# Later weight loads in the scan, rows two experts ahead, doubled columns, no fillers: six edits to a fused scan, expert and DFT kernel

## The chip, the cores and the metric

The kernel runs on one core of a Trainium2 chip, in one launch. The time is device microseconds of that core. Three runs of the kernel before took 473.55, 471.59 and 469.82 us (median 471.59); the execution whose profile is read here took 473.05, of which 471.3 lie between the first and the last instruction.

## The reference

Three stages follow one another (4 batches, 768 positions, 256 features):

```python
# 1. decaying scan, 8 heads of 32, state of 16, in chunks
M = einsum('bhin,bhjn->bhij', C, B) * exp(cum_i - cum_j) * causal
y = M @ x + (C @ state) * exp(cum)
state = exp(sum(la)) * state + sum_j(B_j x_j * exp(cum_last - cum_j))
# 2. mixture of 8 experts; the choice is sticky along a sequence
e = argmax(logits[b, s]) if s == 0 or sigmoid(x @ w_local) < 0.5 else prev_e
out[b, s] = softmax(logits)[e] * (relu(x @ w1[e]) @ w2[e])
# 3. real part of a 2-D DFT, residual, layer norm, feed-forward layer
u = x + real(fft(fft(x, axis=1), axis=2))
un = (u - mean(u)) / sqrt(var(u) + 1e-6)
result = u + relu(un @ w_ch1) @ w_ch2
```

All of it is float32. The kernel keeps that precision by splitting each matmul operand into a high and a low part, so that one product is three matmuls.

## The kernel before

**The scan** (`phase_a`) runs 12 iterations `i`, six chunks of 128 positions by two pairs of batches; ScalarE's `x1t` (L452) closes an iteration. SP issues the chunk loads (`load`, L242, two chunks ahead), GpSimd builds operands and scatters finished rows into `xs_buf` by expert. In the same program loop SP issues the first expert's weights: `load_w(0)`, `r1` at `i = 5` and `r2` at `i = 7`, and at `i = 9` the tables `fa` and `fb` for the DFT. The order in the program is the order on each engine; SP waits only where a buffer is still in use.

**The experts** (`experts`) are taken in turn, the first of which has one early block of 256 rows and then a block of 128. `ffn` has eight f-groups (L847, 48 matmuls; ScalarE takes the relu `hh`, L851, and DVE the rest `hl`, L852), then a block of 24 matmuls (L860) for each 128 rows; GpSimd scatters the result to `y_tok`. PSUM holds three f-groups. After each f-group (0 to 7) and each row block (8 and up), `hook(i)` puts in work for what comes next: the split of the next expert's weights (`w1h`, `w2h` on ScalarE, `w1l`, `w2l` on DVE, L183 and L186), the transposes `tp` of its rows (L874, hook 7), and the preparation of the last stage's weights, `prep_wch`: a load `rawc`, four DVE operations (L133 to L136), a copy on ScalarE (L140) and two operations on GpSimd. `rawc` and the raw expert weights `r` share two buffers of one pool (`wraw`). `load_x` loads the rows `xn` of the next expert, which come from `xs_buf`, or `xs_part` for the last one. That one is sorted again on the way (`sort_rows`) and runs in two pieces, a block of 128 rows and the rest.

**The transform** follows in the same program. At the turn from the last expert, TensorE computes the DFT of the first batch (`f` L1217, `cps` L1231, `mix` L1247 and L1248). Between these stand fillers, matmuls of 512 columns on `fa` with no reader:

```python
keep_clock(ps1, WARM)   # WARM = 10
stage_a(0, 1)
...
keep_clock(ps1, 5)
```

A filler shows as two records in the trace. Six groups of 512 rows go through the feed-forward layer, while the table `plan` says after which f-group of which group the steps of the next batch (fold on DVE, then `mid`: DFT, residual, norm) are taken.

Of the kernel before, what the change touches and what calls it, by code (L numbers as in the profile page):

```python
# [7 lines left out]
FP32 = mybir.dt.float32  # L8
# [9 lines left out]
NE, F = 8, 1024  # L18
# [9 lines left out]
RW = D + 9  # L28
# [7 lines left out]
)  # L36
GATE = -1.5 * 2.0 ** -23

WARM = 10
CA = {}  # L40
_o = 0
for _n, _w in (
# [10 lines left out]
def tile_kernel(ctx: ExitStack, tc: tile.TileContext, io):  # L53
    nc = tc.nc
    V, A, G, PE, SP = nc.vector, nc.scalar, nc.gpsimd, nc.tensor, nc.sync
# [18 lines left out]
    fa = const.tile([128, 12, 128], FP32, name="fa")  # L74
    fb = const.tile([128, 2, 129], FP32, name="fb")
# [33 lines left out]
    def prep_wch(i, pool):  # L109
        n = 512  # L110
        w = i // 4
        q = i % 4
        if w == 0:
            src = io["wc1"][(q // 2) * 128:(q // 2) * 128 + 128, (q % 2) * n:(q % 2 + 1) * n]
            dst = [t[:, q // 2, (q % 2) * n:(q % 2 + 1) * n] for t in wch[0:2]]
            sh = [128, n]
            raw = wraw.tile([128, n, 2], I32, tag="raw", name="rawc")
            SP.dma_start(out=raw.rearrange("p f t -> p (f t)"), in_=src.bitcast(I32))
        else:
            src = io["wc2"][q * 256:q * 256 + 256, :]  # L120
            dst = [t[:, 2 * q:2 * q + 2, :] for t in wch[2:4]]
            sh = [128, 2, D]
            raw = wraw.tile([128, n, 2], I32, tag="raw", name="rawc")
            SP.dma_start(
                out=raw.rearrange("p (k d) t -> p k (d t)", k=2),
                in_=src.bitcast(I32).rearrange("(k p) d -> p k d", p=128),
            )
            dst = [t.rearrange("p k d -> p (k d)") for t in dst]
        hw, lw = raw[:, :, 1], raw[:, :, 0]
        v = pool.tile([128, n], I32, tag="cv", name="cv")  # L130
        e = pool.tile([128, n], I32, tag="ce_", name="ce_")
        r = pool.tile([128, n], FP32, tag="cr", name="cr")
        V.tensor_scalar(out=e, in0=hw, scalar1=3, scalar2=0x3FFFFFF8, op0=ALU.logical_shift_left, op1=ALU.bitwise_and)  # L133
        V.scalar_tensor_tensor(out=v, in0=hw, scalar=-0x40000000, in1=e, op0=ALU.bitwise_and, op1=ALU.bitwise_or)
        V.tensor_scalar(out=e, in0=v, scalar1=-0x800000, scalar2=None, op0=ALU.bitwise_and)
        V.scalar_tensor_tensor(  # L136
            out=r, in0=lw.bitcast(mybir.dt.uint32), scalar=2.0 ** -52, in1=e.bitcast(FP32), op0=ALU.mult, op1=ALU.mult
        )
        vf = v.bitcast(FP32)
        A.activation(out=dst[0], in_=vf, func=ACTF.Copy)  # L140
        ef = e.bitcast(FP32)
        G.tensor_tensor(out=ef, in0=vf, in1=dst[0], op=ALU.subtract)
        G.tensor_tensor(out=dst[1], in0=ef, in1=r, op=ALU.add)
# [11 lines left out]
            )  # L155
        return regs[j]

    def load_w(e, part=None, static=False):

        i = bass.ds(e if static or e == 0 else expert(e), 1)  # L160
        if part != 1:
            r1 = wraw.tile([128, 2, F], FP32, tag="raw", name="r1")
            SP.dma_start(out=r1, in_=io["w1"][i].rearrange("o (k p) f -> p (o k) f", p=128))
            raws[e, 0] = r1
        if part != 0:
            r2 = wraw.tile([128, 8, D], FP32, tag="raw", name="r2")
            SP.dma_start(out=r2, in_=io["w2"][i].rearrange("o (k p) d -> p (o k) d", p=128))
            raws[e, 1] = r2

# [39 lines left out]
    def keep_clock(pool, n):  # L209

        wps = pool.tile([128, 512], FP32, tag="mm1", name="wps")
        for _ in range(n):
            PE.matmul(out=wps, lhsT=fa[:, 0, :], rhs=fa[:, 0:4, :].rearrange("p n k -> p (n k)"), start=True, stop=True)  # L213
# [7 lines left out]
    def phase_a():  # L221
        with ExitStack() as st:
# [467 lines left out]
            for i, (c, bp) in enumerate(pairs):  # L690
# [7 lines left out]
                if i < 4:  # L698
                    zfill(2 * i)
                    zfill(2 * i + 1)  # L700
                if i in (5, 7):
                    ws = load_w(0, i // 7)
                if i == 9:
                    SP.dma_start(out=fa, in_=io["fa"].rearrange("p (n k) -> p n k", k=128))
                    SP.dma_start(out=fb, in_=io["fb"].rearrange("p (n k) -> p n k", k=129))
                    SP.dma_start(out=rix, in_=io["rix"])
# [130 lines left out]
    def ffn(pools, e, xt_src, evac, hook=lambda i: None, n=CAP):  # L837
        hp, ps1, ps2 = pools
# [4 lines left out]
        for f in range(8):  # L843
            ps = ps1.tile([128, CAP], FP32, tag="mm1", name="mm1")
            terms = [(w, xh, d) for d in range(2) for w in (w1h, w1l)] + [(w1h, xl, d) for d in range(2)]
            for k, (w, x, d) in enumerate(terms):
                PE.matmul(  # L847
                    out=ps[:, 0:n], lhsT=w[:, d, f * 128:(f + 1) * 128], rhs=x[:, d, 0:n], start=(k == 0), stop=(k == 5)
                )
            hf = hh[:, f, 0:n]  # L850
            A.activation(out=hf, in_=ps[:, 0:n], func=ACTF.Relu)  # L851
            V.scalar_tensor_tensor(out=hl[:, f, 0:n], in0=ps[:, 0:n], scalar=0.0, in1=hf, op0=ALU.max, op1=ALU.subtract)  # L852
            hook(f)
# [26 lines left out]
    def load_x(pools, e, xn=None):  # L880

        n = -(-CAPS[e] // 128) * 128
        if xn is not None:
            src = xs_buf.rearrange("(e t) r -> e t r", e=NE)[bass.ds(expert(e), 1), 0:n, :]
            SP.dma_start(out=xn[:, 0:n // 128], in_=src.rearrange("o (t p) r -> p (o t) r", p=128))
            return xn
        xn = pools[0].tile([128, 4, RW], FP32, tag="xn", name="xn")
        if e in SORTED:
            src = xs_part[e][0:n, :].rearrange("(t p) r -> p t r", p=128)
        elif e:  # L890
# [98 lines left out]
    def overflow(pools, nr):  # L989
# [4 lines left out]
        with tc.For_i(1, nr, 1):  # L994
            V.tensor_scalar(out=ro, in0=ro, scalar1=float(CAP), scalar2=None, op0=ALU.add)
            for e in range(NE):
# [3 lines left out]
                past(oo, ro, cnt[:, e:e + 1].to_broadcast([128, 4]))  # L1000
                oi = sm.tile([128, 4], I32, tag="oi", name="oi")
                V.tensor_scalar(out=oi, in0=ro, scalar1=float(e * NTOK), scalar2=None, op0=ALU.add)
                xn = pools[0].tile([128, 4, RW], FP32, tag="xn", name="xn")
                for t in range(4):
                    G.indirect_dma_start(
                        out=xn[:, t, :], out_offset=None, in_=xs_buf,
# [17 lines left out]
    def experts():  # L1024
# [19 lines left out]
                nxt = split_x(pools, xn, out_of[:, 0, :], CAPS[0])  # L1044

        moe_expert(pools, 0, xe, ids_e, early, first, n=EARLY)
        last = NE - 1
        for e in range(NE):
            cur = (xn, *nxt)
            more = e < last  # L1050
            if more:
                xn = load_x(pools, e + 1)

            def hook(i):
                nonlocal nxt, ws, nr
# [11 lines left out]
                if more and i in at:  # L1067
                    next(ws, None)
                    if i == at[-1]:
                        next(ws, None)  # L1070
                        ws = load_w(e + 2) if e + 2 < NE else None
                if i == 7 and more:
                    nxt = split_x(pools, xn, out_of[:, e + 1, :], CAPS[e + 1])
                if (e, i) == (0, 5):
                    prep_wch(0, sm)
                if i == 8 and 0 < e < last:
                    prep_wch(e, sm)
                if (e, i) == (last - 1, 11):
                    prep_wch(7, sm)

# [46 lines left out]
    def transform(lead):  # L1127
# [257 lines left out]
        load_z(1)  # L1385
        sq = sm.tile([128, 1], FP32, tag="sq", name="sq", bufs=1)
        A.activation(out=sq, in_=ident[:, 0:1], func=ACTF.Sqrt)
        keep_clock(ps1, WARM)
        stage_a(0, 1)
        correct(0)  # L1390
        for k2 in range(4):
            stage_b(0, k2)
        keep_clock(ps1, 5)
        for k in range(4):
            add_rows(0, k, G if k else V)
        add_mix(0, 0)
        for k in range(1, 5):
# [13 lines left out]
        run(1, 1)  # L1411

        plan = {
# [3 lines left out]
        }  # L1417
        for g, b in ((2, 2), (3, 3)):
            for k, v in (
# [132 lines left out]
```

## Time and profile before

| | us |
|---|---|
| three runs | 473.55, 471.59, 469.82 |
| profiled execution | 473.05 |
| its span, first to last instruction | 471.3 |
| TensorE busy (PE) | 432.4 (92%) |
| VectorE (DVE) / ScalarE (ACT) / GpSimd (POOL) busy | 274.5 / 183.7 / 152.7 |
| mean granted TensorE clock | 0.955 |

The scan fills the span to about 98 us, the experts to 288, the transform the rest. An engine's busy time says little by itself; the chain of waits follows the last instruction back from releaser to releaser, and the windows give busy time and granted clock of a stretch (1.00 is 2.4 GHz, 0.50 is 1.2 GHz). "PE" are matmuls, "SPq" the DMA issues of SP.

### The profile page before, as it was taken

What the parts mean: (1) busy time and instruction counts of PE and PEld (TensorE: products, weight loads), DVE (VectorE), ACT (ScalarE), POOL (GpSimd) and SP (SyncE); (2) the same over time, 40 slices, a digit from 0 to 9 for tenths busy, and PEclk for the clock granted to TensorE, in tenths of its full rate; (3) what the DMA queues carried; (4) which work ended last, traced back from release to release, by engine and by line L of the source; (5) the groups of instructions that cost most, each with busy time, mean ns of one, the idle gap of its engine ahead of it and who ended that gap; (6) DMA issues with size and microseconds to landing.
All of it is one profiled execution on the core that took longest, in us unless ns stands there. A gap on an engine that the chain in (4) does not pass through costs nothing.

```text
span 471.3 us, 8949 instructions
## 1 busy us (share of the span) xinstructions
PE 432.4 (92%) x3455; PEld 379.0 (80%) x3455; DVE 274.5 (58%) x738; ACT 183.7 (39%) x407; POOL 152.7 (32%) x195
## 2 busy tenths in 40 slices
PE   8798688799899999987989999989999999999996
PEld 4576565469779898986979996668989899998986
DVE  5677577664675657656464453494664578564241
ACT  2354344424344545645353232333240443333130
POOL 2247745431205280622414322342601361400000
PEclk9999799799789999999898799999999999999999
DMA  8799501127364455457351042300131200010101
GB/s 273 258 325 328 186 25 49 66 74 259 116 208 158 148 196 185 149 190 234 118 198 63 19 146 64 139 22 2 56 124 35 78 25 23 2 47 0 46 3 49
DMA packets 33372, 55.22 MB, mean 117 GB/s; under 512 B 3240, under 2 KB 22473, under 8 KB 33320
## 3 DMA queue, kind: packets, MB, share of 16 engines
q1 hardware_dynamic: 29800, 46.28, 29.9%
q0 software_dynamic: 3008, 8.00, 4.9%
q8 instruction: 29, 0.48, 0.4%
q10 hardware_dynamic: 512, 0.28, 0.2%
q14 instruction: 23, 0.19, 0.1%
HBM read 42.05 MB, written 12.63 MB: 116 GB/s over the span
## 4 chain that ended last, share of the span: by engine, by line
PE 78%; DVE 7%; DMA 6%; ACT 5%; issue 2%; another core or an unknown queue 1%; SPq 0%; ACTq 0%
PE mm L860 30%; PE mm L847 23%; PE tl L498 4%; PE wps L213 3%; DMA xn<-xs_buf 3%; PE tp L874 3%; PE g L414 2%; PE f L1217 2%; PE yb L445 2%; DMA xn<-xs_part 2%; PE mb L262 2%; ACT x1t L452 1%; PE yb L434 1%; PE g L262 1%; PE cps L1231 1%
## 5 line engine op out<-in xcount | busy, mean ns | idle before, releaser
L852 DVE SCALAR_TENSOR_TENSOR hl<-mm,hh 128x512 fp32r<-128x512 f32 (+9 forms) x128 | 70.1, 562 | 55.4 <-ACT hh L851 54.6
L851 ACT ACTIVATE hh<-mm 128x512 fp32r<-128x512 f32 (+9 forms) x128 | 62.5, 495 | 83.3 <-PE mm L847 83.1
L860 PE MATMUL mm<-w2h,hh 128*128 128x256 f32 (+3 forms) x224 | 65.5, 292 | 0.0
L860 PE MATMUL mm<-w2l,hh 128*128 128x256 f32 (+3 forms) x224 | 64.3, 287 | 0.0
L860 PE MATMUL mm<-w2h,hl 128*128 128x256 f32 (+3 forms) x224 | 64.3, 287 | 0.0
L961 POOL DMA_INDIRECT y_tok<-y,ids x26 | 32.7, 1257 | 91.2 <-ACT y L960 70.0
L847 PE MATMUL mm<-xh,w1h 128*128 128x128 f32 (+8 forms) x160 | 52.3, 335 | 3.6 <-DVE hl L852 2.8
L860 PE MATMUL mm<-c2h,hh 128*128 128x256 f32 x192 | 54.5, 284 | 0.0
L860 PE MATMUL mm<-c2h,hl 128*128 128x256 f32 x192 | 53.8, 280 | 0.0
L860 PE MATMUL mm<-c2l,hh 128*128 128x256 f32 x192 | 53.8, 280 | 0.0
L847 PE MATMUL mm<-xh,w1l 128*128 128x128 f32 (+8 forms) x160 | 51.5, 330 | 0.0
L860 PEld LDWEIGHTS mm<-w2h,hh 128*128 128x128 f32 (+3 forms) x224 | 42.2, 188 | 0.1
L847 PE MATMUL mm<-xl,w1h 128*128 128x128 f32 (+8 forms) x160 | 40.4, 334 | 1.9 <-DVE xl L877 1.9
L860 PEld LDWEIGHTS mm<-w2l,hh 128*128 128x128 f32 (+3 forms) x224 | 42.1, 188 | 0.1
L860 PEld LDWEIGHTS mm<-w2h,hl 128*128 128x128 f32 (+3 forms) x224 | 41.9, 187 | 0.2
L847 PE MATMUL mm<-xh,c1h 128*128 128x512 f32 x96 | 39.5, 411 | 0.6 <-ACT xh L876 0.6
L847 PE MATMUL mm<-xh,c1l 128*128 128x512 f32 x96 | 38.0, 396 | 0.0
L186 DVE TENSOR_TENSOR w2l<-r,w2h 128x1024 fp32r<-128x1024 f32 (+1 forms) x18 | 21.7, 1212 | 27.5 <-ACT w2h L183 27.5
L847 PEld LDWEIGHTS mm<-xh,w1h 128*128 128x128 f32 x160 | 31.6, 197 | 7.1 <-DVE hl L852 5.0
L860 PEld LDWEIGHTS mm<-c2l,hh 128*128 128x128 f32 x192 | 36.4, 190 | 0.1
L860 PEld LDWEIGHTS mm<-c2h,hh 128*128 128x128 f32 x192 | 36.3, 189 | 0.1
L860 PEld LDWEIGHTS mm<-c2h,hl 128*128 128x128 f32 x192 | 36.0, 188 | 0.0
(279 smaller groups left out, 866.2 us busy)
## 6 DMA issues: line engine op xcount, KB each, us to landing
r<-in_w_dram SPq DMA_DIRECT2D x16, 1024.0 KB
rawc<-in_wc_dram SPq DMA_DIRECT2D x8, 512.0 KB
out_dram<-o SPq DMA_DIRECT2D x24, 128.0 KB
home<-y_tok SPq DMA_DIRECT2D x3, 768.0 KB
xs_buf<-scr SPq DMA_DIRECT2D x8, 265.0 KB
c1h<-in_x_dram SPq DMA_DIRECT2D x4, 512.0 KB
home<-y_tok SPq DMA_DIRECT2D x4, 512.0 KB
xn<-xs_buf SPq DMA_DIRECT2D x3, 530.0 KB
```

Source lines behind the costliest of these rows:

```text
L186: V.tensor_tensor(out=l_[:, x:y], in0=r_[:, x:y], in1=h[:, x:y], op=ALU.subtract)
L213: PE.matmul(out=wps, lhsT=fa[:, 0, :], rhs=fa[:, 0:4, :].rearrange("p n k -> p (n k)"), start=True, stop=True)
L262: PE.matmul(out=ps[:, 0:w], lhsT=wrm[:, 0:128], rhs=wrm[:, 0:w], start=True, stop=True)
L414: PE.matmul(out=gp[q][:, u].rearrange("p h i -> p (h i)"), lhsT=lds[c]["bt"][r:r + 32, 2 * bp + u, :], rhs=ch[r:r + 32, u].rearrange("p q ...
L445: PE.matmul(out=yb[32 * h:32 * h + 32, g, 128 * u:128 * u + 128], lhsT=xts[i][:, u, 4 * g + h, :], rhs=m[:, u, 4 * g + h, :], start=(c == ...
L498: PE.matmul(out=tl[:, 128 * g:128 * g + 137], lhsT=x1t[:, g, u, :], rhs=ca[:, o:o + 137], start=(g == 0), stop=(g == 1), skip_group_check= ...
L847: PE.matmul(out=ps[:, 0:n], lhsT=w[:, d, f * 128:(f + 1) * 128], rhs=x[:, d, 0:n], start=(k == 0), stop=(k == 5))
L851: A.activation(out=hf, in_=ps[:, 0:n], func=ACTF.Relu)
L852: V.scalar_tensor_tensor(out=hl[:, f, 0:n], in0=ps[:, 0:n], scalar=0.0, in1=hf, op0=ALU.max, op1=ALU.subtract)
L860: PE.matmul(out=ps[0:m, :], lhsT=h[:, f, t * 128:t * 128 + m], rhs=w[:, f, :], start=(k == 0), stop=(k == 23))
L874: PE.transpose(ps[d][:, t * 128:(t + 1) * 128], src(t, d), ident)
L961: w = G.indirect_dma_start(out=y_tok, out_offset=bass.IndirectOffsetOnAxis(ap=ids[0:m, t:t + 1], axis=0), in_=y[0:m, :], in_offset=None, b ...
```

## The change

It has six parts.

1. In the scan, `load_w(0)` moves from `i = 5, 7` to `i = 6, 8`, and it, `fa` and `fb` are held: GpSimd writes one element of the target buffer in its own order, and the DMA waits for that write.
2. `load_x(e + 2)` is issued at the start of expert `e`, where `load_x(e + 1)` was; the pool has three such buffers for it.
3. In a 128-row `ffn`, each L847 matmul streams its 128 columns twice, into 256 columns of PSUM; only the first 128 are read.
4. `prep_wch(0)` leaves expert 0; 0 to 5 are taken one expert later than 0 to 6 were, and 6 joins expert 1, ahead of `load_w(3)`.
5. At the turn, the first ten fillers go, and five become four.
6. In `plan`, the first step of `mid(1)` moves from after f-group 3 to after f-group 4 of group 0; all twelve are taken by (0, 9) as before.

```diff
@@ prep_wch
-        r = pool.tile([128, n], FP32, tag="cr", name="cr")
+        r = pool.tile([128, n], FP32, tag="cr", name="cr", bufs=1)
@@
+    def held(t):
+        G.memset(t, 0.0)
+
-    def load_w(e, part=None, static=False):
+    def load_w(e, part=None, static=False, late=False):
@@ after each of r1 and r2 is allocated, before its DMA
+            if late:
+                held(r1[0:1, 0, 0:1])
@@ phase_a
-                if i in (5, 7):
-                    ws = load_w(0, i // 7)
+                if i in (6, 8):
+                    g = load_w(0, i // 8, late=True)
+                    ws = g if i == 6 else ws
                 if i == 9:
+                    for t in (fa[0:1, 0, 0:1], fb[0:1, 0, 0:1]):
+                        held(t)
@@ ffn
+            q = 2 if n == 128 else 1
                 PE.matmul(
-                    out=ps[:, 0:n], lhsT=w[:, d, f * 128:(f + 1) * 128], rhs=x[:, d, 0:n], start=(k == 0), stop=(k == 5)
+                    out=ps[:, 0:q * n].rearrange("p (q n) -> p q n", q=q), lhsT=w[:, d, f * 128:(f + 1) * 128],
+                    rhs=x[:, d, 0:n].unsqueeze(1).to_broadcast([128, q, n]), start=(k == 0), stop=(k == 5),
                 )
@@ load_x
-        xn = pools[0].tile([128, 4, RW], FP32, tag="xn", name="xn")
+        xn = pools[0].tile([128, 4, RW], FP32, tag="xn", name="xn", bufs=3)
@@ experts
         moe_expert(pools, 0, xe, ids_e, early, first, n=EARLY)
+        xn1 = load_x(pools, 1)
         for e in range(NE):
             if more:
-                xn = load_x(pools, e + 1)
+                xn = xn1
+            if e + 2 < NE:
+                xn1 = load_x(pools, e + 2)
@@ hook
                         next(ws, None)
+                        if e == 1:
+                            prep_wch(6, sm)
                         ws = load_w(e + 2) if e + 2 < NE else None
-                if (e, i) == (0, 5):
-                    prep_wch(0, sm)
                 if i == 8 and 0 < e < last:
-                    prep_wch(e, sm)
+                    prep_wch(e - 1, sm)
@@ transform
-        keep_clock(ps1, WARM)
         stage_a(0, 1)
-        keep_clock(ps1, 5)
+        keep_clock(ps1, 4)
@@ plan
-            (0, 0): ((1, 0, 1),), (0, 1): ((1, 0, 1), (1, 1, 1)), (0, 2): ((1, 1, 1),), (0, 3): ((1, 2, 1),),
-            (0, 4): ((1, 2, 2),), (0, 5): ((1, 2, 1),), (0, 6): ((1, 2, 1),), (0, 7): ((1, 2, 2),),
-            (0, 8): ((1, 2, 3),), (0, 9): ((1, 2, 2),), (1, 0): ((1, 2, 1),), (1, 1): ((1, 2, 1),), (1, 3): ((1, 2, 1),),
+            (0, 0): ((1, 0, 1),), (0, 1): ((1, 0, 1), (1, 1, 1)), (0, 2): ((1, 1, 1),), (0, 4): ((1, 2, 1),),
+            (0, 5): ((1, 2, 2),), (0, 6): ((1, 2, 1),), (0, 7): ((1, 2, 2),), (0, 8): ((1, 2, 3),),
+            (0, 9): ((1, 2, 3),), (1, 0): ((1, 2, 1),), (1, 1): ((1, 2, 1),), (1, 3): ((1, 2, 1),),
```

The lines of the kernel after stand 7 to 15 further down. On SP, from the end of the scan's loads on, before (`r` are expert weights, `L242` chunk loads):

```order
L163 DMA r_698<-in_w_dram 128x2x1024
L242 DMA c2h<-in_ct_dram 128x512
L242 DMA c2h<-in_bt_dram 128x512
L242 DMA c1l<-in_x_dram 128x1024
L242 DMA c2l<-in_bn_dram 128x512
L167 DMA r_916<-in_w_dram 128x8x256
L704 DMA fa<-in_fa_dram 128x1536
L705 DMA fb<-in_fb_dram 128x258
L706 DMA rix<-in_rix_dram 128x8
```

and with the change:

```order
L249 DMA c2h<-in_ct_dram 128x512
L249 DMA c2h<-in_bt_dram 128x512
L249 DMA c1l<-in_x_dram 128x1024
L249 DMA c2l<-in_bn_dram 128x512
L168 DMA r_814<-in_w_dram 128x2x1024
L174 DMA r_1021<-in_w_dram 128x8x256
L714 DMA fa<-in_fa_dram 128x1536
L715 DMA fb<-in_fb_dram 128x258
L716 DMA rix<-in_rix_dram 128x8
```

The four loads of the last chunk now stand ahead of both weight loads.

On DVE, at the end of expert 1 and the start of expert 2, before:

```order
L133 TENSOR_SCALAR ce__1998<-rawc 128x512
L134 SCALAR_TENSOR_TENSOR cv<-rawc,ce__1998 128x512
L135 TENSOR_SCALAR ce__1998<-cv 128x512
L136 SCALAR_TENSOR_TENSOR cr<-rawc,ce__1998 128x512
L186 TENSOR_TENSOR w2l<-r_1858,w2h 128x1024 x2
L852 SCALAR_TENSOR_TENSOR hl<-mm_2114,hh 128x448
L899 SCALAR_TENSOR_TENSOR tk<-xu,out_of 128x4
L913 TENSOR_SCALAR lead<-tk 128x4
L852 SCALAR_TENSOR_TENSOR hl<-mm_2127,hh 128x448
```

and with the change:

```order
L132 TENSOR_SCALAR ce__1995<-rawc 128x512
L133 SCALAR_TENSOR_TENSOR cv<-rawc,ce__1995 128x512
L134 TENSOR_SCALAR ce__1995<-cv 128x512
L135 SCALAR_TENSOR_TENSOR cr<-rawc,ce__1995 128x512
L193 TENSOR_TENSOR w2l<-r_1852,w2h 128x1024 x2
L132 TENSOR_SCALAR ce__2073<-rawc 128x512
L133 SCALAR_TENSOR_TENSOR cv<-rawc,ce__2073 128x512
L134 TENSOR_SCALAR ce__2073<-cv 128x512
L135 SCALAR_TENSOR_TENSOR cr<-rawc,ce__2073 128x512
L864 SCALAR_TENSOR_TENSOR hl<-mm_2123,hh 128x448
```

The four operations of the second `prep_wch` (L132 to L135) stand between `w2l` and the first `hl` of expert 2.

On SP, at the end of expert 0 and in expert 1, before (a TENSOR_LOAD reads the number of an expert):

```order
L163 DMA r_1856<-in_w_dram 128x2x1024
L167 ISA
L167 DMA r_1858<-in_w_dram 128x8x256
L895 ISA
L895 DMA xn<-xs_buf 128x4x265
L152 TENSOR_LOAD who
L885 ISA
L885 DMA xu<-xs_buf 128x4x265
L118 DMA rawc<-in_wc_dram 128x1024
L152 TENSOR_LOAD who
L163 ISA
L163 DMA r_2076<-in_w_dram 128x2x1024
```

and with the change:

```order
L168 DMA r_1850<-in_w_dram 128x2x1024
L174 ISA
L174 DMA r_1852<-in_w_dram 128x8x256
L151 TENSOR_LOAD who
L907 ISA
L907 DMA xn<-xs_buf 128x3x265
L151 TENSOR_LOAD who
L897 ISA
L897 DMA xu<-xs_buf 128x4x265
L117 DMA rawc<-in_wc_dram 128x1024
L123 DMA rawc<-in_wc_dram 128x2x512
L168 ISA
L168 DMA r_2082<-in_w_dram 128x2x1024
```

`xn` of expert 3 now comes ahead of `rawc`, and a second `rawc` ahead of `r`.

## Rows read from the trace of the kernel before

**Rows 1.** The page, part 4: shares of the chain of waits that ended last.
```profile
PE 78%; DVE 7%; DMA 6%; ACT 5%; issue 2%; another core or an unknown queue 1%; SPq 0%; ACTq 0%
```

**Rows 2.** Windows: stretch, length, busy us (count) per engine, granted clock, DMA share, GB/s.
```profile
44.40:53.30 8.90, 5.06 (x94) 3.61 (x90) 5.24 (x18) 3.14 (x9) 6.45 (x10) 1.00 0.87 316
53.30:61.60 8.30, 7.59 (x93) 5.86 (x93) 4.83 (x12) 2.82 (x8) 4.98 (x8) 0.59 0.14 49
61.60:68.20 6.60, 5.00 (x101) 3.60 (x90) 5.06 (x18) 4.09 (x10) 2.58 (x4) 1.00 0.01 2
118.00:125.00 7.00, 7.00 (x36) 7.00 (x36) 2.79 (x5) 0.52 (x2) 0.00 (x0) 0.51 0.24 77
...
224.00:227.30 3.30, 2.72 (x13) 2.75 (x14) 0.95 (x3) 1.03 (x2) 0.00 (x0) 0.50 0.12 46
...
264.90:271.70 6.80, 6.80 (x34) 6.80 (x33) 0.87 (x3) 0.83 (x3) 0.32 (x1) 0.50 0.00 0
288.00:305.50 17.50, 17.50 (x74) 10.28 (x73) 4.85 (x22) 5.75 (x16) 4.90 (x11) 1.00 0.39 122
```

**Rows 3.** Chain of waits (start us, us, work): 256-row block; last expert 128-row block.
```profile
101.15 6.42 PE mm L847 x48
107.56 2.83 PE mm L860 x24
...
267.42 4.85 PE mm L860 x24
```

**Rows 4.** Chain of waits, expert 0 with its 128-row block.
```profile
113.44 3.31 PE mm L847 x30
...
119.28 4.26 DMA rawc<-in_wc_dram
...
125.30 0.42 ACT hh L851 x2
...
126.70 1.73 DVE w2l L186
128.43 1.14 DVE ids L899
...
130.76 11.14 PE mm L847 x43
```

**Rows 5.** Timeline of DVE, experts 1 and 2: start us, us of one or more instructions.
```profile
152.51 1.23 DVE L186 TENSOR_TENSOR w2l<-r,w2h 128x1024 fp32r<-128x1024 f32 x1 [1.44 <-ACT w2h L183]
...
165.51 0.15 DVE L899 SCALAR_TENSOR_TENSOR ids<-xn,out_of 128x3 int32<-128x3 int32 x1
```

**Rows 6.** Timeline of ACT, second f-group of expert 2.
```profile
156.60 1.05 ACT L183 ACTIVATE w1h<-r 128x1024 fp32r<-128x1024 f32 x1
```

**Rows 7.** Waits of PE, 98 to 310 us: total us, times, longest.
```profile
PE tp L874 <- DMA xn<-xs_buf: 4.9, 2, 3.3
...
PE tp L874 <- DMA xn<-xs_part: 2.2, 1, 2.2
```

**Rows 8.** Chain of waits from the last expert into the transform.
```profile
288.12 8.58 PE wps L213 x20
...
301.17 4.29 PE wps L213 x10
305.46 0.90 PE tp L874 x7
```

**Rows 9.** Timeline of ACT at the turn.
```profile
288.69 1.28 ACT L1387 ACT_TABLE_LOAD   x1
```

**Rows 10.** Chain of waits, first group of the transform: PE is released by this.
```profile
314.64 0.21 DVE home L1178
...
326.46 1.38 PE mm L847 x6
```

**Rows 11.** Chain of waits in the scan: the steps without a known releaser.
```profile
51.32 1.96 another core or an unknown queue
...
81.67 2.50 another core or an unknown queue
```

More of the change, by code (lines that the diff above doesn't have):

```diff
@@ L37 @@
 GATE = -1.5 * 2.0 ** -23
-WARM = 10
 CA = {}
@@ L166, in load_w @@
             r2 = wraw.tile([128, 8, D], FP32, tag="raw", name="r2")
+            if late:
+                held(r2[0:1, 0, 0:1])
             SP.dma_start(out=r2, in_=io["w2"][i].rearrange("o (k p) d -> p (o k) d", p=128))
@@ L1002, in overflow @@
                 V.tensor_scalar(out=oi, in0=ro, scalar1=float(e * NTOK), scalar2=None, op0=ALU.add)
-                xn = pools[0].tile([128, 4, RW], FP32, tag="xn", name="xn")
+                xn = pools[0].tile([128, 4, RW], FP32, tag="xn", name="xn", bufs=3)
                 for t in range(4):
```

## The prediction, before the run

> **What bounds the kernel now.** I read the chain of waits first, then the windows at each place where the chain leaves TensorE, then the timelines there. The chain is 78% TensorE [rows 1]: a change pays where it takes out a step of the chain that is not matmul, or a stretch in which the matmuls run at the lower clock. The windows [rows 2] show both. In the scan, 44.4 to 53.3, TensorE is busy 5.06 of 8.90 us and the DMA engines 87% of the time, with 0.59 of the clock just after; 118 to 125, 224 to 227.3 and 264.9 to 271.7 run at 0.50, the 1.2 GHz level, and three stretches of 3.4 us like the second start at 131.7, 247.8 and 316.1. A matmul block of 24 takes 4.85 us at that level and 2.83 at full clock [rows 3], so each us of such a stretch holds about half a us that could come back.
>
> The profiled execution took 473.05 us, 1.5 more than the median of 471.59. The sum is made against 473.05.
>
> **Expert 0: the first `prep_wch` leaves.** Its load is issued when DVE has freed the buffer, and DVE then stands in front of it: from 119.28 (`rawc`, 4.26) to 125.30, where the last two relus run [rows 4], are 6.02 us. What takes its place is the last f-group, which needs the DVE product that ends there: 6 matmuls at 3.31/30 = 0.11 us, and a relu, 0.95 together. GpSimd's two tensor operations of the prep go too; beside them `w2l` took 1.73 and `ids` 1.14 [rows 4] where later experts show 1.23 and 0.15 [rows 5]: 1.5 more, if that is why. 6.02 - 0.95 + 1.5 = 6.6. The half-clock stretch after the idle time (3.4 us from 131.7) is worth 1.7. If the stretch of 118 to 125 stays, the row block costs 2 of this back, so the ends are 4.6 and 8.3; I take **8.0**, since DVE's wait is what emptied TensorE.
>
> **Expert 1 to 2: prep 6 arrives.** Eight preps remain eight; 1 to 5 keep their places as 0 to 4. Prep 6 stands behind `w2l`, its load issued when prep 0 frees the buffer, some 5 us before DVE gets there, so I cost its landing at nothing. It adds four DVE operations (2.2 us beside row blocks) and moves `load_w(3)`'s first half from that buffer to the one that `w2l` frees, at 153.74 [rows 5]. ScalarE cuts that half into `w1h` at 156.60 [rows 6]; a load that lands 4.3 us after issue, as the 512 KB of `rawc` did, or 6, since 512 KB more take 1.7 at the 316 GB/s of the scan [rows 2], makes it 1.4 to 3.1 late. Behind `w1h` on ScalarE stand the relus, and TensorE can run two f-groups of some 1.2 us ahead on three PSUM buffers. Cost 0 to 4, with a clock loss behind it; I take **-1.2**.
>
> **Rows two experts ahead.** PE's transposes wait 4.9 us in two places for `xn` from `xs_buf` and 2.2 in one from `xs_part` [rows 7]. Issued an expert earlier, each load has over 20 us of cover, and in SP's queue nothing new stands behind it that is due sooner: its third buffer has been free for an expert. All 7.1 go, and with them the two half-clock stretches behind the idle times (224 [rows 2] and 247.8), 1.7 each: **+10.5**, between 7.1 and 10.5.
>
> **128-row blocks streamed twice.** 96 matmuls grow from 128 to 256 columns. The 128-column ones are 0.110 apart [rows 4]; at 256 columns the rows show 2.83/24 = 0.118 and 6.42/48 = 0.134 [rows 3]. So 96 x 0.008 to 0.024 is 0.8 to 2.3 lost, nearer the lower end because the second figure holds the start of its block; half of it lies in expert 0. In the last expert, 264.9 to 271.7 at 0.50 [rows 2] begins inside such a block after a wait for DVE; if the denser stream holds the clock, 3.4 come back. If not, only the loss stays. I take **+2.4**, between -2.3 and 2.6. The Trainium skill (TensorE: Matmul & The Clock Gate, section Back-to-back issue gap) gives 134 cycles for 128 columns and 262 for 256 at full clock, an estimate of 53 ns more each and 5 us in all. The rows disagree, with 8 to 24 ns more.
>
> **The turn.** Twenty filler records, 8.58 us, go from the path [rows 8]; TensorE stands at full clock there [rows 2]. The DFT's inputs are ready before 288, and the next limit is ScalarE's table load, 1.28 us from 288.69 [rows 9], which delays the copy of `f` by some 0.5. Of the later fillers one in five goes, 0.86 of 4.29; but the rows for the transposes at 305.46 become ready just then, so that fifth was free. 8.58 - 0.5 = 8.1, plus 0.2 for a little slack: **+8.3**, between 6.4 (a half-clock stretch of 3.4 us follows) and 8.6.
>
> **The plan.** `stage_a(1, 0)` moves behind one more f-group. TensorE is released at 314.85 by DVE's fold [rows 10]. But that f-group needs a PSUM buffer which DVE frees at about the same time, so the wait mostly changes its name: **+0.5**, between -1 (the steps now crowd in front of the next transposes) and 1.7.
>
> **The scan.** 2.9 MB (two loads of 1024 KB, one of 768, one of 129) leave the time before 53 us, when the DMA engines are full. The gap in TensorE at 51.32 (1.96) ends as they drain, but it has no known releaser, and 81.67 has a like one of 2.50 [rows 11] when the scan's loads are long done. Iterations 6 and 7, 44.4 to 53.3 to 61.6, took 17.2 us where iteration 8 takes 6.6 at full clock [rows 2]: 4 to 5 could go, half of it clock. Later landing costs nothing while its cover lasts: `r1` is first cut at the end of iteration 7, and its hold stands in GpSimd's queue in iteration 6, behind two scatters; `r2` and `fa` have two iterations and more. If `r1` went only at the end of iteration 6, 53.3, it would land some 4.3 to 6 later, still within iteration 7. I take **+3.0**, between 0 and 6.
>
> 8.0 - 1.2 + 10.5 + 2.4 + 8.3 + 0.5 + 3.0 = 31.5, and 473.05 - 31.5 = **441.5**. Against the median it could be 1.5 lower; I leave that for small waits not seen. All low ends together give 4.6 - 4 + 7.1 - 2.3 + 6.4 - 1 + 0 = 10.8, or 462; all high ends 8.3 + 0 + 10.5 + 2.6 + 8.6 + 1.7 + 6 = 37.7, or 435.
>
> **The rivals.**
> (a) *The clock does not come back.* The stretches move instead of vanishing: 1.7 + 3.4 + 3.4 = 8.5 of the sum are clock, and a stretch at expert 2 and one at the turn would take 3.4 more: 441.5 + 8.5 + 3.4 = 453, or 449 with part of it. For it: every one of these stretches follows a wait, and new waits come. Against: most of the waits before them go. 0.21, of which 0.03 with so many new waits that less than 1% is gained.
> (b) *The scan was slow by DMA alone*, and the plan's stretch goes as well: 441.5 - 3 - 1.2 = 437, down to 434. The second gap with idle rings speaks against it. 0.11.
> (c) *A doubled matmul costs its columns.* At 512 columns six take 1.38 [rows 10], 0.230 each; by the slope from 0.118, 0.056 per 128 columns, 96 cost 5.4 instead of 1: 446. The 0.110 at 128 columns, far above half of 0.118, speaks against it. 0.05. This is the way that the Trainium skill's rule above would go.
> (d) *Slower: the turn without its fillers leaves TensorE at half clock into the transform.* A block of 24 then costs 2.02 more [rows 3]. Losing the 31.5 and 5 more takes 18 such blocks, some 87 us at the lower level; the longest stretch in the rows is 6.8. It decides only if the clock stays down for most of the 166 us that follow: 441.5 + 36.4 = 478. 0.03. The Trainium skill (TensorE: Matmul & The Clock Gate, section Why this matters for your kernels) advises against idle gaps between matmul bursts, which speaks for fillers; no row shows this turn without them.
> (e) *The holds do nothing*, because the gap at 51.32 was never DMA: 444.5. It lies inside the forecast, which has 0.60 with 437 to 447.
>
> **How the numbers follow.** The range 435 to 453 leaves out the lowest quarter of (b), the upper third of (a), and (d), under 0.2 together. A change of 1% (4.7 us) is about what these runs can tell. Faster is all but (d) and the tail of (a): 0.94; same 0.03; slower 0.03.
>
> **What would show it.** In the profile after: no DVE wait for `rawc` in expert 0 and expert 1 starting near 124 less what the scan gave; no wait of the transposes for `xn`; clock 1.00 through the last expert's 128-row block; transposes 17.3 - 8.3 = 9 us after the last expert's final matmul; at expert 2 a late `w1h` of 1 to 4 us; scan iterations 4 to 7 near 6 us each. I am wrong if half-clock stretches stand behind new places, if `w1h` of expert 2 stops TensorE for over 4 us, or if the scan waits for `r1`.

## The result, and the profile after

| | before | change |
|---|---|---|
| runs beside each other, us | 469.37 to 473.55, median 470.70 | 443.98, 448.41, 449.04, 451.18, median 448.73 |
| ratio | | 0.9492 [0.9399, 0.9585] |
| profiled execution, us | 473.05 | 449.04 |
| its span, us; granted clock | 471.3; 0.955 | 447.2; 0.977 |
| another chip (C below), median us | 462.34 | 438.13, ratio 0.9529 [0.9469, 0.9589] |

The ratios here and below leave out runs of either kernel that lie over 1.5% above its fastest one, so they differ from the quotient of the medians, and ratios from different chips cannot be compared.

The kernel is 22 us faster, where 30 were forecast against the median. The spans differ by 24.1, and the question is where the missing 7 are. The page's shares of the chain, which answer to [rows 1], show what has left: DMA fell from 6% to 1%.

```profile
PE 79%; DVE 8%; ACT 6%; issue 3%; DMA 1%; another core or an unknown queue 1%; POOL 1%; ACTq 0%; DVEq 0%
```

The chain of waits of the changed kernel (start us, us, work; L858, L872, L886 are the old L847, L860, L874) answers to [rows 3, 4, 8]. From the early block to the transform:

```profile
104.65 6.19 PE mm L858 x48
...
116.67 1.45 PE mm L858 x12
...
118.36 1.07 ACT w1h L190
...
119.51 1.22 DVE w1l L193
...
127.13 10.40 PE mm L858 x48
137.53 0.88 PE tp L886 x8
...
149.61 5.51 DMA r<-in_w_dram
...
161.97 0.66 PE tp L886 x6
...
183.26 0.66 PE tp L886 x6
...
217.87 0.88 PE tp L886 x8
...
236.62 0.88 PE tp L886 x8
...
251.24 3.85 PE mm L858 x30
255.09 2.81 PE mm L872 x24
257.90 6.32 PE mm L858 x48
...
269.82 1.34 PE f L1232 x12
...
273.97 1.34 PE f L1232 x12
...
283.07 0.56 PE tp L886 x3
```

The chain has no `rawc` in expert 0, no `xn` at the last transposes and no filler between 273.97 and 283.07, and a block of 24 in the last expert's 128 rows takes 2.81 instead of 4.85. One DMA step is new: the weights `r` of expert 3, issued at 149.61, landing 5.51 later and cut within expert 2. PE's waits from 98 to 310 us (us in total, times, longest) no longer have the two `xn` lines of [rows 7]; the longest are now:

```profile
PE mm L858 <- DVE hl L864: 4.0, 6, 1.6
PE ps L934 <- DVE ahead L929: 1.5, 1, 1.5
```

`ahead` is a vector operation in expert 2, part of sorting the last expert's rows. Before, this wait was short, and one of expert 1 for the low part of its rows (`xl`) stood there that is gone now:

```profile
PE mm L847 <- DVE xl L877: 1.9, 1, 1.9
...
PE ps L922 <- DVE ahead L917: 0.3, 1, 0.3
```

The table goes by stretches of the chain, between events that both kernels have (us; a plus is a gain). The second pair of traces was taken later, before and change on one chip (C); that execution of the kernel before was faster than the eleven others of it there.

| stretch | forecast | first pair | second pair |
|---|---|---|---|
| start to early block | +3.0 | 101.15 to 104.65: -3.5 | 90.20 to 93.29: -3.1 |
| to expert 1's transposes for expert 2 | +8.0 | 40.75 to 32.88: +7.9 | 38.24 to 32.87: +5.4 |
| two experts on | -1.2 | 43.42 to 45.73: -2.3 | 43.53 to 45.66: -2.1 |
| to the last expert's transposes | +10.5, in part in the next row | 61.23 to 53.36: +7.9 | 58.78 to 53.16: +5.6 |
| to the first DFT | +2.4 | 37.50 to 33.20: +4.3 | 36.23 to 33.22: +3.0 |
| DFT to transposes (the turn) | +8.3 | 21.41 to 13.25: +8.2 | 21.41 to 13.24: +8.2 |
| the rest | +0.5 | 165.84 to 164.13: +1.7 | 164.41 to 164.06: +0.4 |
| sum | 31.5 | 24.1 | 17.3 |

The stretches at the 1.2 GHz level add up to 40.9 us in the trace before and 20.4 in the one after (14.0 to 17.4, 55.0 to 61.8, 89.1 to 99.3: all in the scan). At most half of such a stretch is lost, so at most 10.2 of the 24.1 are clock. In the second pair it is 13.7 against 6.8, at most 3.4 of 17.3. Taken off in full, that leaves 13.9 us in both pairs; the rest of a pair's gain may be clock.

### The profile page after: what moved, and what is told of

It is laid out like the page before. It is cut to its first block, busy times and chain, and to the rows that moved or that the text cites. A ratio compares the mean times of both kernels' runs of the same rounds, so it can differ in the third digit from the quotient of the medians.

```text
span 447.2 us, 8888 instructions
## 1 busy us (share of the span) xinstructions
PE 415.7 (93%) x3433; PEld 366.6 (82%) x3433; DVE 272.9 (61%) x738; ACT 184.0 (41%) x407; POOL 151.9 (34%) x199
## 4 chain that ended last, share of the span: by engine, by line
PE 79%; DVE 8%; ACT 6%; issue 3%; DMA 1%; another core or an unknown queue 1%; POOL 1%; ACTq 0%; DVEq 0%
PE mm L872 30%; PE mm L858 27%; PE tl L505 4%; PE g L421 3%; PE tp L886 2%; PE f L1232 2%; PE yb L452 2%; PE mb L269 2%; PE g L269 1%; ACT x1t L459 1%; PE yb L441 1%; DMA r<-in_w_dram 1%; PE cps L1246 1%; DVE hl L864 1%
## 5 line engine op out<-in xcount | busy, mean ns | idle before, releaser
L872 PE MATMUL mm<-w2h,hh 128*128 128x256 f32 (+3 forms) x224 | 63.3, 283 | 0.0
L872 PE MATMUL mm<-w2h,hl 128*128 128x256 f32 (+3 forms) x224 | 62.6, 279 | 0.0
L872 PE MATMUL mm<-w2l,hh 128*128 128x256 f32 (+3 forms) x224 | 62.5, 279 | 0.0
L872 PE MATMUL mm<-c2h,hh 128*128 128x256 f32 x192 | 54.5, 284 | 0.4 <-DVE o L1344 0.4
L858 PE MATMUL mm<-xh,w1h 128*128 128x256 f32 (+7 forms) x160 | 51.2, 329 | 3.1 <-DVE hl L864 2.4
L872 PE MATMUL mm<-c2l,hh 128*128 128x256 f32 x192 | 53.6, 279 | 0.0
L872 PE MATMUL mm<-c2h,hl 128*128 128x256 f32 x192 | 53.6, 279 | 0.0
L858 PE MATMUL mm<-xh,w1l 128*128 128x256 f32 (+7 forms) x160 | 49.8, 320 | 0.0
L858 PE MATMUL mm<-xh,c1h 128*128 128x512 f32 x96 | 39.0, 406 | 2.2 <-DVE hl L864 1.6
L872 PEld LDWEIGHTS mm<-w2l,hh 128*128 128x128 f32 (+3 forms) x224 | 39.6, 177 | 0.1
L872 PEld LDWEIGHTS mm<-w2h,hh 128*128 128x128 f32 (+3 forms) x224 | 39.6, 177 | 0.1
L872 PEld LDWEIGHTS mm<-w2h,hl 128*128 128x128 f32 (+3 forms) x224 | 39.5, 176 | 0.2
L858 PE MATMUL mm<-xl,w1h 128*128 128x256 f32 (+7 forms) x160 | 38.4, 321 | 0.0
L858 PE MATMUL mm<-xh,c1l 128*128 128x512 f32 x96 | 37.5, 391 | 0.0
L872 PEld LDWEIGHTS mm<-c2h,hh 128*128 128x128 f32 x192 | 36.1, 188 | 0.8 <-DVE o L1344 0.6
L872 PEld LDWEIGHTS mm<-c2l,hh 128*128 128x128 f32 x192 | 36.1, 188 | 0.1
L872 PEld LDWEIGHTS mm<-c2h,hl 128*128 128x128 f32 x192 | 36.1, 188 | 0.0
L858 PEld LDWEIGHTS mm<-xh,w1h 128*128 128x128 f32 x160 | 30.2, 188 | 6.8 <-DVE hl L864 5.4
```

Of the source, the lines that this page charges most:

```text
L858: PE.matmul(out=ps[:, 0:q * n].rearrange("p (q n) -> p q n", q=q), lhsT=w[:, d, f * 128:(f + 1) * 128], rhs=x[:, d, 0:n].unsqueeze(1).to_b ...
L872: PE.matmul(out=ps[0:m, :], lhsT=h[:, f, t * 128:t * 128 + m], rhs=w[:, f, :], start=(k == 0), stop=(k == 23))
```

## The experiments

The experiments ran on three chips. Runs of the kernel before had a median of 471.29 us on chip A, like those above, of 462.15 on chip B and of 462.34 on chip C. Times from different chips are therefore compared by stretches of the trace.

### The holds and the scan

```diff
-                if i in (6, 8):
-                    g = load_w(0, i // 8, late=True)
-                    ws = g if i == 6 else ws
+                if i in (5, 7):
+                    ws = load_w(0, i // 7)
@@
-                    for t in (fa[0:1, 0, 0:1], fb[0:1, 0, 0:1]):
-                        held(t)
```

> The change without its part on the scan: the first expert's weights and the tables are issued at iterations 5, 7 and 9 as before, without the holds. Theory (the holds buy nothing, and what the scan lost in the profile of the change was the clock, which differs from run to run): the median stays within 2 us of the change's 448.7, the scan's iterations 4 to 7 take 29.5 us as in both profiles, and the gap of 2 us at iteration 6 stays. Rival A (the prediction's: full DMA rings slow the scan): 3 to 6 us slower, 452 to 455. Rival B (the late loads themselves cost the scan the 3.5 us): 445.

449.03 us (447.21 to 450.66) on chip A, ratio 0.9654 [0.9580, 0.9728]: the change's time within its spread. The pause of iteration 6 is there in both. Iterations 4 to 7 take 30.80 us, not the 29.5 expected; 10.2 us of half clock lie there, where both traces of the first pair have 6.8. Chain of waits without the holds:

```profile
51.84 1.96 another core or an unknown queue
53.88 0.61 ACT x1t L459
```

and of the change:

```profile
53.76 2.02 another core or an unknown queue
55.86 0.61 ACT x1t L459
...
83.97 2.61 another core or an unknown queue
```

A second try shifted every later TensorE instruction, in case the pauses came from where the program stands in memory:

```diff
+            warm(24, 32)   # 24 small matmuls at the start of the scan
```

> The change with 24 more matmuls of 32 columns, on zeros and without a reader, at the start of the scan, to shift what follows in TensorE's instruction stream by some 96 instructions. For the two gaps of the scan that have no releaser (about 2.0 us at iteration 6 and 2.5 us at iteration 10, at the same place of the program in all six traces so far). Theory (they hang on the place in TensorE's instruction stream): both move to another iteration, or vanish. Rival (they hang on what the iterations do, the scatters of GpSimd for one, or on data): both stay at iterations 6 and 10.

It took 452.57 us in its one execution, and the pauses were gone. But it ran on chip B, and there they are gone in every trace, those with the unshifted program too. It tells nothing of the shift. Nor is it clear that TensorE was the engine to shift. In both pauses the profile shows ScalarE standing still, here in the kernel before, though the matmuls that it reads from had ended at 51.00 and 81.99 (in brackets its idle time; "remote" is a releaser that the profile does not know):

```profile
53.36 0.60 ACT L452 ACTIVATE x1t<-yb 128x512 f32<-128x512 f32 x1 [2.04 <-remote]
...
84.19 0.17 ACT L557 ACTIVATE f__1272<-mb 128x4 f32<-128x4 f32 x1 [2.53 <-remote]
```

So the change and the kernel before were run with a trace each on chip C:

> The changed kernel itself, unaltered, to be compared with the three other runs of this call on one chip. If the change's gain is the same everywhere, the ratio to the kernel before is 0.94 to 0.96. If the scan's two pauses (2.0 us at iteration 6, 2.6 us at iteration 10) belong to the chip and not to the program, they are there or not there alike in this run and in the kernel before of this call.

> The kernel before, for its trace on the same chip as the changed one. Theory (the pauses in the scan come with the chip or the execution, not with what the rings carry): its scan shows the pauses where the changed kernel's does, and the scan's length differs from the changed kernel's by no more than a half-clock stretch (3.4 us times a half each) explains. Rival (the rings' load makes them): the pauses are in this kernel and not in the changed one.

The change took 438.13 us (437.24 to 440.17). The kernel before took 454.56 in the one execution profiled, and 462.34 in the median of the eleven beside it (456.42 to 465.31). Neither trace has a pause: from the fourth `x1t` to the eighth, the four iterations 4 to 7, pass 24.05 us before and 24.08 after. In the first pair they took 29.70 and 29.49. The windows of iteration 6 (length, busy us (count) of PE, PEld, DVE, ACT, POOL, granted clock, DMA share, GB/s) settle what the rings have to do with it. The kernel before, chip C:

```profile
43.20:49.90 6.70, 4.90 (x100) 3.51 (x90) 5.73 (x19) 3.05 (x9) 5.76 (x10) 1.00 1.06 383
```

the change, same chip:

```profile
44.20:50.90 6.70, 4.84 (x96) 3.52 (x90) 5.72 (x19) 3.04 (x10) 5.76 (x11) 1.00 0.46 107
```

the change, first pair:

```profile
46.87:55.86 8.99, 5.00 (x95) 3.61 (x90) 5.16 (x18) 3.14 (x9) 6.60 (x12) 0.95 0.59 179
```

With the DMA engines at 1.06 the iteration takes 6.70 us, with 0.46 the same 6.70, and with 0.59 in the first pair 8.99. The load of the rings does not make the pause, and taking it away buys nothing; the traces of the first pair and of chip A have the pauses, none from chips B and C. What makes them was not found.

The scan's loss of 3.5 and 3.1 us begins ahead of the holds. In the first pair the change is 2.4 us late at the first `x1t` (16.56 before, 18.95 after) and still 2.4 at the end of the second pause. Of these, 0.7 are the first loads (the first six matmuls of the chain take 4.80 us before and 5.49 after), and the other 1.7 the half-clock stretch from 14.0. In the second pair it is 0.95 late at the first `x1t` (4.27 and 5.21 us for the six) and 0.97 at 80 us. What is left, 1.1 and 2.1 us, is lost where the half-clock stretch at the scan's end lies: 10.2 us with the change and 6.8 before in the first pair, 6.8 and none in the second. The kernel with the fillers back (below), whose scan is that of the change, starts its early block at 92.07, 1.2 earlier, with 3.4 us of half clock there. On chip A the kernel without the holds starts it at 102.96, three others with them at 101.80, 105.09 and 105.82, one sooner and two later. Whether they have a hand in the stretch at the scan's end stays open: it measures 10.2 us in all four traces with pauses and holds and 6.8 in the two without holds; on chips B and C it measures 0 to 6.9 in six with them (the shifted kernel aside), and the one without has none.

### Rows two experts ahead, undone

```diff
-        xn1 = load_x(pools, 1)
@@
-                xn = xn1
-            if e + 2 < NE:
-                xn1 = load_x(pools, e + 2)
+                xn = load_x(pools, e + 1)
```

> The change with the rows loaded one expert ahead, as before. Theory (a wait for the rows and the clock it costs): the waits of the transposes for the rows return, 7 us, with two half-clock stretches, 9.4 us slower than the change, 458. Rival (the rows would land in time now that other loads have moved): no more than 2 us slower.

455.21 us (449.37 to 456.28) on chip A, ratio 0.9745 [0.9618, 0.9871], some 6 us more than the change, where 9.4 were expected. PE's waits, 98 to 310 us, have the two lines again:

```profile
PE tp L886 <- DMA xn<-xs_buf: 2.8, 2, 1.7
PE tp L886 <- DMA xn<-xs_part: 1.3, 1, 1.3
```

The three steps cost 4.1 us of waiting, and the stretch to the last transposes 57.6 instead of 53.4, 4.2 more, with no half-clock stretch in it. So the wait is what this part removes, and the clock comes on top in some executions.

### Doubled columns, undone

```diff
-            q = 2 if n == 128 else 1
+            q = 1
```

> The change with the 128-row blocks streamed once. Theory (the dense stream keeps the clock in the last expert's block): a half-clock stretch of 3.4 to 6.8 us returns there and the kernel is 1 to 3 us slower, less some 1 us that the columns cost: 450 to 452. Rival (the clock held because the waits ahead of the block are gone): no half-clock stretch, and 1 us faster, 447.7, since 96 matmuls go back from 0.12 to 0.11 us.

449.21 us (446.69 to 454.13) on chip A, ratio 0.9662 [0.9541, 0.9784]: as a time, no difference that these runs can tell, and less than the 450 to 452 expected. The windows of the last expert's 128-row block show what is behind it:

```profile
247.60:250.30 2.70, 2.69 (x24) 2.70 (x25) 1.05 (x5) 0.83 (x3) 2.46 (x2) 1.00 0.04 10
250.30:253.70 3.40, 3.40 (x18) 3.40 (x18) 0.75 (x3) 0.55 (x2) 0.00 (x0) 0.50 0.00 0
```

With single columns TensorE is busy without a break and the granted clock still drops to 0.50 in the middle of the block; with doubled columns this block is at 1.00:

```profile
251.24:257.90 6.66, 6.66 (x56) 6.66 (x57) 1.79 (x7) 1.39 (x5) 2.48 (x2) 1.00 0.02 4
```

The block takes 8.0 us single (247.61 to 255.61), 6.66 doubled, 9.58 before. One trace could be chance, but all agree: the granted clock drops within this block in the three traces with single columns (this one and both of the kernel before) and in none of the eleven with doubled ones. Against a block with no half-clock stretch the doubling costs little: the last expert's 30 matmuls of the chain took 3.85 us, 0.128 each, where single ones took 0.110 [rows 4], so some 0.9 for the 48 of a block.

### The seventh preparation

Three ways to take prep 6 out of expert 1. First, prep 6 in the old place of prep 7 (end of expert 6), and prep 7 whole inside the last expert's second block:

```diff
-                        if e == 1:
-                            prep_wch(6, sm)
@@ (last - 1, 11)
-                    prep_wch(7, sm)
+                    prep_wch(6, sm)
@@ rest, i == 7, ahead of the fold
+                prep_wch(7, sm)
```

> The change with the second preparation of expert 1 (number 6) moved to the end of expert 6, and number 7 from there into the last expert's second block. Theory (its buffer makes the load of expert 3's first weights 7 us late): that load is issued at the first buffer's release again, the wait of 5.5 us in the chain goes, and the kernel is 2.5 to 3 us faster, 446. Rival (the four vector operations between the weights and the first relu parts of expert 2 are what costs): the wait for the load goes but a wait for VectorE takes its place at the end of expert 6 or in the last expert, and the time stays within 1 us of 448.7.

455.61 us (451.75 to 457.82) on chip A, ratio 0.9771 [0.9674, 0.9869]: slower than the change. The stretch from expert 1's start to the transposes behind it gained 1.6 us, but prep 7's load left late:

```profile
262.20 6.69 DMA rawc<-in_wc_dram
...
276.43 2.93 PE f L1230 x12
```

In SP's queue it stood behind the loads of `home`; the fold behind it on DVE was late, and the DFT `f` ran at the lower clock (2.93 instead of 1.34). Second, prep 7's load issued early, only its vector operations left there:

```diff
+                    prep_wch(7, sm, 0)     # (last - 1, 11): the load alone
@@ rest, i == 7, ahead of the fold
+                prep_wch(7, sm, 1)     # the operations
```

> The change with number 6 of the preparations moved to the end of expert 6, and number 7 split: its load issued there too, its vector operations taken in the last expert ahead of the fold. Theory: expert 2 starts without the wait for its weights (as in the run before this one, 1.6 us there), and the load of number 7 is long there when its operations run, so that the wait of 6.7 us that the run before had there is gone: 1 to 2 us faster than the change, 447. Rival (vector work in the last expert delays the fold, and with it the DFT): a wait of TensorE for the fold of 1 to 3 us takes the gain away, 448 to 450.

439.87 us (437.76 to 441.84), ratio 0.9668 [0.9548, 0.9789], on chip B, where the change itself wasn't run (without its last four fillers, below, it took 437.64 there). From expert 1's transposes to expert 2's 22.70 us, where the change has 24.44: the wait for `r` is gone. So is that for `ahead`, 0.2 instead of 1.5, and this try cannot tell the two apart. Four operations of DVE in front of the fold still made it late:

```profile
253.52 0.69 DVE cr L142
254.21 2.05 DVE home L1183 x2
256.28 1.51 DVE home L1189
...
259.36 2.93 PE f L1238 x12
```

Third, these operations in DVE's pause while the last expert's 128 rows go through their second product:

```diff
+        def pause(i):
+            if i == 7:
+                prep_wch(7, sm, 1)
-        moe_expert(pools, last, *lead, n=128)
+        moe_expert(pools, last, *lead, pause, n=128)
```

> The eighth table's load stays where the change has the preparation of the eighth (end of the seventh expert), its vector operations (2.2 us) go into the pause of 3.4 us that VectorE has in the last expert's second product of the 128 block, and the seventh's preparation takes the eighth's old place. Theory (the seventh table's transfer in the second expert delays the weights for the fourth): the stretch from the second expert's transposes to the third's falls from 24.4 us to about 22.8, and nothing is late at the fold, so the run is 1.5 to 2 us faster than the changed kernel of this call. Rival (VectorE's operations of the eighth are late at the fold again, as when they stood at the eighth step of the second block): the first DFT waits some 1.5 us and the sum is no better than the changed kernel.

437.03 us (435.87 to 437.57) beside the change's 438.13 (437.24 to 440.17) on the same chip C; ratios 0.9494 [0.9437, 0.9551] and 0.9529 [0.9469, 0.9589]. It is the best of the kernels run beside the change, by 1.1 us, which these runs barely tell. The stretch is 22.82 us against 24.34, as expected, and TensorE's wait for `ahead` is short again:

```profile
PE ps L941 <- DVE ahead L936: 0.2, 1, 0.2
```

But most of the 1.5 is lost again at the fold, by an engine that neither theory named. The chain of waits there:

```profile
245.06 1.30 POOL ce__3359 L148
...
247.88 2.44 DMA y_tok<-y,ids
...
250.80 3.82 DMA home<-y_tok
...
254.64 0.57 DVE home L1183
...
257.32 1.79 PE f L1238 x12
```

GpSimd's two operations of prep 7 stand in front of its scatter of the block's rows, which the load of `home` needs.

### The turn without fillers, and the plan

```diff
+        keep_clock(ps1, 10)
         stage_a(0, 1)
@@
-        keep_clock(ps1, 4)
+        keep_clock(ps1, 5)
```

> Part 5 undone: ten fillers ahead of the turn's second DFT and five behind its four products, as before. Theory (the fillers stand in the path, and the clock does not fall without them): the turn goes from 9.1 us to 17.0 to 17.4, and the run is 7.5 to 8.5 us slower than the changed kernel of this call. Rival (they pay for themselves later by the clock): a half-clock stretch less behind the turn, so 5 to 6.5 us slower.

445.15 us (444.21 to 447.33), ratio 0.9687 [0.9624, 0.9750], 7.0 more than the change on the same chip C. Its chain has the fillers back:

```profile
260.82 8.59 PE wps L220 x20
...
273.88 4.29 PE wps L220 x10
278.17 0.90 PE tp L886 x7
```

The turn takes 17.35 instead of 9.09, 8.3 us more; up to it this execution was 1.5 faster (the scan's clock, above) and behind it 0.8 slower, with no half-clock stretch in either: 443.0 - 435.5 = 7.5. The rival would have needed one less behind the turn. The last four fillers were then taken away too:

```diff
-        keep_clock(ps1, 4)
```

> The change without the last four fillers at the turn. Theory (they only fill a wait for ScalarE and VectorE): the turn takes the same 9.1 us, and the median stays within 2 us of 448.7. Rival (they keep the clock): a half-clock stretch of 3.4 us or more at the start of the transform, 1.7 us or more slower in the profile.

437.64 us (436.18 to 440.42) on chip B, ratio 0.9620 [0.9504, 0.9736]. The turn stayed at 9.11 us, so these four cost nothing there. A half-clock stretch of 3.4 us followed at 273.9, as the rival had it, but the first group took 30.10 nevertheless (30.04 in the change). And the plan put back:

```diff
-            (0, 0): ((1, 0, 1),), (0, 1): ((1, 0, 1), (1, 1, 1)), (0, 2): ((1, 1, 1),), (0, 4): ((1, 2, 1),),
+            (0, 0): ((1, 0, 1),), (0, 1): ((1, 0, 1), (1, 1, 1)), (0, 2): ((1, 1, 1),), (0, 3): ((1, 2, 1),),
```

> The change with the plan of the transform's first group as before. From the first transposes of the transform to those of its second group the kernel before took 31.75 us with a half-clock stretch of 3.4 us in it, the change 30.04 without one. Theory (the 1.7 us were the clock, which the wait for the rows and the fillers ahead set): about 30 us with the old plan too. Rival (the plan's step is what saved it): 31 to 32 us, with a wait for the fold ahead of the DFT and perhaps the half-clock stretch again.

435.55 us in one execution on chip B. From the turn's transposes to those of the next group pass 29.77 us with the old plan (269.72 to 299.49), 30.04 with the new, and 31.75 before, where a half-clock stretch lay at 316.1. The 1.7 us of the first pair are that stretch and not the plan. With the old plan TensorE waits for the fold, as it does not in the change:

```profile
PE f L1232 <- DVE home L1193: 1.7, 1, 1.7
```

Its waits for `hl` add up to 2.4 us instead of 4.0: the wait has changed its name, as forecast.

## Why the prediction was right, and which step failed

**The turn** (8.3): 8.2 in both pairs, and 8.3 by putting the fillers back. Rival (d), the lower clock into the transform, did not come. But the limit that was named for the fillers' place, ScalarE's table load, costs nothing. It does delay the copy of `f`, which ends by 276.53 (ACT):

```profile
274.54 1.28 ACT L1402 ACT_TABLE_LOAD   x1
...
275.95 0.58 ACT L1236 ACTIVATE home<-f 128x512 f32<-128x512 f32 x1
```

TensorE is busy until just then, and `mix` follows `cps` without a gap, as it did before (chain):

```profile
275.31 1.23 PE cps L1246 x12
276.55 0.33 PE mix L1262 x2
```

So from the last expert's end to `mix` the whole 8.6 us are won. From there to the transposes 6.5 us pass instead of 6.2: TensorE now waits for the rows, which go through ScalarE, GpSimd and DVE, and no longer for the end of the fillers. That the 0.5 charged for the table load came near to this is luck.

**Rows two experts ahead** (10.5): the waits went whole. In the second pair they were 4.5 and 1.2 us, and the stretch gained 5.6; in the first 7.1. The clock on top is what varies: 3.4 were forecast, 2.3 is what the first pair leaves when the 7.1 are taken from the 9.4 that this part gained there (7.9, and 1.5 from the last transposes to the 128-row block). In the second pair, and in the kernel with this part undone, there was none.

**Doubled columns** (2.4): the last expert's block gained 2.9 us in the first pair. The clock held where a dense single stream did not hold it, and the loss per matmul was of the forecast size. Rival (c) is out: it asked for 0.056 more per matmul, and 0.018 were measured.

**Expert 0** (8.0): 7.9 and 5.4 for the stretch, early block and expert 1 included. DVE's wait for `rawc` is gone as forecast. Expert 1's first matmul comes 3.4 and 2.9 us sooner after the start of the 128 block (127.18 before, 126.97 after in the first pair), and from it to expert 1's transposes pass 4.2 and 2.4 us less: 14.72 and 12.99 before, 10.56 in both traces of the change. In both pairs the wait for `xl` behind DVE is gone there. The 1.7 by which the two traces of the kernel before differ is the half-clock stretch from 131.7, which only the first has. So the clock was worth its 1.7 where it fell, and without it the part gave 5.9 and 5.3, where 6.6 was forecast. No experiment put this part back by itself; it rests on the two pairs.

**Prep 6** (-1.2): the size was 2.0 and 1.8 us, inside the 0 to 4 given, and taking it out gives 1.5 to 1.7 back. The mechanism was right by half. Expert 3's weights came late behind the extra `rawc`, as forecast: `w1h` stood 17.6 us behind expert 1's transposes, 14.7 before. But TensorE's longest stop there is the 1.5 us for `ahead`, which ends at 154.73 and thus ahead of that `w1h` at 155.14. What pushes it back are the four operations of the prep on DVE and its copy on ScalarE, in front of the relu and `hl` of expert 2; the prediction saw these operations and put no price on them. The late weights then stop TensorE for only some 0.3. Taken away alone, either might leave the other as the limit; the experiments took both away.

**The plan** (0.5): the trace before ran into a half-clock stretch here; without it the plan is worth 0.4 in one pair and less than nothing against the old plan alone.

**The scan** (3.0) is the step that failed. The prediction read the 0.87 of the DMA engines beside the gap at 51.32 as its cause. Rival (e) was right as far as the runs show: the holds win nothing. The evidence against it lay in the rows already, as the prediction noted: the second gap, long after the scan's loads [rows 11]. It should have cut the term to zero, not halved it. In the term's place the runs showed a loss of 3.5 and 3.1 us: 0.7 and 0.9 from the first loads, which the change does not touch and which vary among traces of the same scan (4.34 to 5.49 us for the first six matmuls), and the rest from half-clock stretches, one of them in a new place at the scan's start.

**The sum.** Of the 7.4 us between 31.5 and 24.1 the scan alone is 6.5. The rest is small errors of both signs. In the second pair the gap is 14.2, and most of what is missing beside the scan's 6.1 is clock that the kernel before had not lost there. Rival (a) held in part: the stretches at the lower level were halved, and those left all stand in the scan, 20.4 us where the trace before has 13.7. That carried the median of 448.73 from the 441.5 towards (a)'s 453, not past it.

## What to carry to other kernels

A full DMA queue beside an idle engine is no cause until the engine waits for something in that queue: look for a second pause of the same kind where the queue is empty, and believe that one. Price a removed wait by its own length, and keep the clock behind it as a separate term that one execution has and the next has not. Work that is moved out of one engine's way is paid on every engine that it uses: here each new place for one preparation met another queue (SP's, DVE's, GpSimd's).

## What the runs showed that was not expected

The same program has two pauses, of 2.0 and 2.5 to 2.6 us, in the scan in the six traces of the first pair and chip A, and none in the eight of chips B and C. The early block starts at 101.15 to 105.82 us in the traces with pauses and at 90.20 to 93.54 in those without (the shifted kernel aside, whose first `x1t` comes at 30.35 us). That is more than the holds were ever thought to give. And the granted clock can drop to 0.50 within a stretch in which TensorE is busy throughout (250.3 to 253.7 above, after 2.7 us of unbroken matmuls at 1.00), while the same block with columns doubled stays at 1.00.
